# A planner for attention beside a long convolution counts TensorE's instructions in groups of 256 and holds convolution lags and fillers back by that count

## The chip, the core and the metric

The kernel runs on one core of a Trainium2 chip. A core has five engines that run their own instruction streams and meet at semaphores: TensorE (matrix multiply, PE in the profile; its weight loads are listed apart as PEld), VectorE (DVE), ScalarE (ACT), GpSimd (POOL) and SyncE (SP, used here to start DMA transfers). The metric is device microseconds (us) of one execution, lower is better. The time before is the median of three runs.

## The reference

Two independent parts are computed and laid side by side. Part A is attention over 2048 positions with 32 heads of width 16; part B is a gated convolution, in which every one of 512 channels is convolved with its own filter of 2048 taps:

```python
def _A_ref(x, wqkv, wo):            # x 2048 x 512, H = 32, Dh = 16
    qkv = (x @ wqkv)                # split into q, k, v by head
    scores = einsum("bhqd,bhkd->bhqk", q, k) * Dh ** -0.5
    o = einsum("bhqk,bhkd->bhqd", softmax(scores), v)
    return o.reshape(B, S, D) @ wo

def _B_ref(q, k, v, shift_k, ssm_k, ssm_D):   # each 2048 x 512
    k_shift = sum over t < 4 of k delayed by t, times shift_k[:, t]
    kv = k_shift * v
    y = causal convolution of kv with ssm_k, channel by channel (by FFT)
    return q * (y + kv * ssm_D)

out = concatenate([a, b], axis=-1)            # 2048 x 1024, bf16
```

## The kernel before

**Attention.** The scores are cut into 2048 blocks of 128 keys by 512 queries of one head. A score matmul (line 676) makes one block in a PSUM bank; it uses 32 of the 128 rows of the array, so up to four of different rows run together. The planner's unit of time is a step T: the score matmuls of two or three blocks, and one ScalarE instruction (line 709) that takes the exponential of those blocks at once and writes them to the ring PT. Some of the blocks, 277 of the 2048, take another way: VectorE makes their exponentials from integer arithmetic in four instructions of 512 columns (lines 751, 758 twice, 763). The blocks of step T-2 are then multiplied with the values (line 792), up to four at a time in different columns of the array, into one PSUM bank. A group is 64 blocks; at its end VectorE transposes and divides (lines 853 to 873).

**The convolution.** A channel's filter is laid in SBUF as 128 shifted copies (ring WR, 16 slots of 512 KB, filled by SP's DMAs from a scratch in HBM). Four channels form a "quad"; 128 quads of 16 lags each are computed. One lag is four small matmuls with 128 columns (line 962), one for each channel, which run together in four column strips of the array. So a lag is eight TensorE instructions, four weight loads and four matmuls, and all lags together are 8192 matmuls.

**Other work on TensorE.** Projections of x (q units, line 395; k units, 404; v units, 427), the short convolution (416), output projection (903), transposes of the convolution's result (987), and fillers (1167), matmuls with a zero weight that add nothing and that keep TensorE busy where it would wait. A q unit makes the queries of one head group and 512 positions: two halves of two matmuls, an eviction by VectorE to the single buffer QS (line 443), and eight small DMAs from POOL's queue that spread QS into the ring QT (line 260, 16 KB each). The eviction of the next q unit waits for these eight, as it overwrites QS.

**What sets the order.** The order of every engine's instructions is fixed when the kernel is built, by a planner written in Python in the same file. Each engine is an object `Eng` with a clock `t`; `Eng.op` adds an instruction (or a run of them), moves the clock by a modelled duration, and notes when its result will be there. `dma` does so for transfers, with a rate (`DMA_KB`) and a latency (`late`). The main loop goes step by step: `emit_qk` (scores and exponential of T), `pv_step` (value products), `emit_bg` (units and convolution lags), `warm_up` (fillers). In `emit_bg` a number of lags is placed that is the least of `LAGS`, a budget `st["lags"]` that grows with planned time (`PACE`, `RATE`), and what fits before the next scores are due (`room`). In `warm_up` fillers are placed up to a modelled gap. The planner's clock before the change knows of engines, semaphores and transfers, and of nothing else.

Of the kernel before, what the change touches and what calls it, by code (L numbers as in the profile page):

```python
# [23 lines left out]
C = 512  # L24
# [9 lines left out]
CHB = 32  # L34
PVB = 6
BGB = 7
N_OPEN = 68
LAGS = 6
PACE = 1.2
KEYS0 = 256  # L40
END = 16

# [16 lines left out]
T_DVE = 6  # L61
SLOT = 16
OPEN = 80
CLOSE = 10
REST = 3
LEN = 3
WIN_D = 2
S_U = 0.5
S_FX = 0.55
S_T = 0.2  # L70
S_C = 0.3
PLAN = 705
JOIN = 0.05
JOIN2 = 0.15
MOST = 3
# [7 lines left out]
BACKLOG = 6.0  # L83
MARGIN = 0.35
SPARE = 0
DMA_KB = 396
X_KB = 200
WINDOW = 3.4
HALF = 0.25
TURN = 0.1  # L90
SOON = 0.5
NEAR = 0.2
FULL = 1.6
BUSY = 0.85
FILL_GAP = 0.2
RATE = 3.7
CAP = 14.0
WAIT = 1.5
LATE = 0.2
# [2 lines left out]
SWITCH = 0.105  # L102
LANDS = 0.115
MM = 0.216
LAG = 0.0555
FILL = 0.054


class Eng:

    def __init__(self, sem, done):
        self.sem = sem
        self.n = 0
        self.ops = []
        self.seen = {}
        self.done = done
        self.t = 0.5
        self.runs = []
        self.kind = None
# [7 lines left out]
    def op(self, fn, deps=(), inc=True, us=(0.06, 0.12), run=0.0, kind=None, lat=0.132):  # L127
        if kind is None:
            self.t = max(self.t + us[0], self.at(deps) + us[1])
        else:  # L130
            self.t = max(self.t + self.turn(kind), self.at(deps) + lat) + run
            self.kind = kind
            self.runs.append((self.t, run))
        waits = []
        for d in deps:
            if d is None:
                continue
            sm, v = d
            if self.seen.get(id(sm), 0) < v:
                self.seen[id(sm)] = v  # L140
                waits.append((sm, v))
        if inc:
            self.n += 1
        self.ops.append((waits, fn, self.sem if inc else None))
        if inc:
            self.done[(id(self.sem), self.n)] = self.t + (LANDS if kind else 0.0)
        return (self.sem, self.n)

    def run(self, e):
        for waits, fn, sm in self.ops:  # L150
            for w in waits:
                e.wait_ge(*w)
            ins = fn(e)
            if sm is not None:
                ins.then_inc(sm, 1)


class DmaSem:
# [10 lines left out]
def bass_concat_heads__mha_block__ssm_conv_h3__prompt_kernel(  # L169
# [17 lines left out]
    def enter(cm):  # L187
        ctxs.append(cm)
        return cm.__enter__()

    def sem(name):
        return enter(nc.semaphore(name))
# [50 lines left out]


    done = {}
    pe, act, dve, pool, sp = [Eng(sem(n), done) for n in ("s_pe", "s_act", "s_dve", "s_pool", "s_sp")]
    dma_t = [0.0]

    def at(*deps):
        return pe.at(deps)  # L250

    def dma(eng, dsem, outp, inp, deps=(), transpose=False, kb=512, rate=DMA_KB, late=3.6):
        h = dsem.add()
        start = max(eng.t, at(*deps))
        dma_t[0] = max(dma_t[0], start + late) + kb / rate
        done[(id(h[0]), h[1])] = dma_t[0]

        def fn(e):
            f = e.dma_start_transpose if transpose else e.dma_start
            f(outp, inp).then_inc(dsem.sem, 16)  # L260
        issue = kb / (rate if rate < DMA_KB else 155) if transpose else 0.55
        eng.op(fn, deps, inc=False, us=(issue, issue + 0.06))
        return h
# [297 lines left out]
    def take_banks(T):  # L561
# [7 lines left out]
        def comes_free(b):  # L569
            if held.get(b) == "w" and (part[0] or T <= win["stop"] and (T < win["begin"] + 2 or near(T, CLOSE))):  # L570
                return False
# [14 lines left out]
        else:  # L586
# [3 lines left out]
            banks = list(range(ends[1], 6))  # L590
        if T >= N_OPEN and near(T, OPEN) and T >= win.get("last", 0) + REST and "bank" not in win and len(banks) > 2 and late["bank"] is None and len(queue) > LAST_BLKS + 18:
            b = hold(T, banks, "w")
# [21 lines left out]
    late = {"bank": None}  # L614
# [108 lines left out]
    def dve_block(T, bl):  # L723
        if len(bl) < 3 or WIN_D and "bank" in win and (part[0] or WIN_D > 1 and near(T, CLOSE)) or T < T_DVE or len(queue) < LAST_BLKS + 3 * (TAIL_GAP - N_LAST) + 3:
            return None
# [281 lines left out]
    units = [("kv", c, i) for c in range(2) for i in range(4)] + [(x, 1, i) for i in range(4) for x in "kv"]  # L1007
    early += [(N_OPEN - 5 - 2 * (len(units) - i), u) for i, u in enumerate(units)]

    def step(n):  # L1010
        return PLAN * n // (NQB * NG)

# [6 lines left out]
    part = [None]  # L1019

    def room(T):
        lim = at(h_exp[min(T, end[0] - 1)]) - 0.47 - MARGIN
        return lim - max(pe.t, at(bank_free[BGB]))

    def next_unit(T):
        if T < N_OPEN:
            return early[0] if early and ready(early[0][1]) else None
# [8 lines left out]
    def unit_step(T):  # L1036
        if T < N_OPEN:
            stop = N_OPEN
        elif "bank" in win:
# [4 lines left out]
        while not tight:  # L1044
# [3 lines left out]
            else:  # L1048
# [3 lines left out]
                due, u = job  # L1052
            if T < N_OPEN:
                bank = PVB if u == ("v", 0, 0) else BGB
# [36 lines left out]
    def emit_bg(T):  # L1091
        st = state
        unit_step(T)
        if T == N_OPEN:
            assert not early
            st["started"], st["t"] = True, pe.t
        if T - end[0] in tail_mm:
            assert st["qd"] == C // 4 and not st["turn"], (T, st)
            for t, g in tail_mm[T - end[0]]:
                op_mm(NQB - 1, t, g, g + 1, tail_bank(t))  # L1100
            return
        if st["qd"] == C // 4 and not st["turn"]:
            if T < end[0] + min(tail_mm) and h_wop[0] is not None:
                bank_free[BGB] = pe.op(keep_busy, [bank_free[BGB], h_wop[0]], run=MM, kind="F")
            return
        if st["turn"] and st["qd"] == C // 4:
            if T < end[0] + min(tail_mm) - 1 and at(h_ybw[0]) > pe.t - 0.2:
                return
            conv_turn(C // 32 - 1, BGB)
            st["turn"] = False  # L1110
            return
        if not st["started"]:
            return
        left_us = max(1.14 * (PLAN - END - T), 1.0)
        st["lags"] = min(st["lags"] + min(PACE * st["left"] / left_us, RATE) * (pe.t - st["t"]), CAP)
        st["t"] = pe.t
        left = min(LAGS, int(st["lags"]), int((room(T) - pe.turn("C") - SWITCH) / LAG))
        while left > 0 and st["qd"] < wr_next[0] and kv_n[st["qd"] // 32] == 4 and at(h_wr[st["qd"]]) + WAIT <= pe.t:
            if st["turn"] and st["qd"] % 4 == 3 and st["lag"] + left >= NB:
                left = NB - 1 - st["lag"]  # L1120
                if left <= 0:
                    break
            n0 = st["lag"]
            if n0 == 0 and st["qd"] % 4 == 0 and at(bank_free[BGB]) > pe.t - 0.2:
                break
            n1 = min(n0 + left, NB)
            left -= n1 - n0
            st["lags"] -= n1 - n0
            st["left"] -= n1 - n0
            conv_lags(st["qd"], n0, n1)  # L1130
            st["lag"] = n1 % NB
            if n1 == NB:
                st["qd"] += 1
                if st["qd"] % 4 == 0:
                    st["turn"] = st["turn"] or st["qd"] % 8 == 0
                    break
# [13 lines left out]
    def warm_up(T):  # L1150
        if T < 1 or T > end[0]:
            return
        while True:
            gap = at(h_exp[T - 1]) + 0.14 - pe.t - FILL_GAP
            lately = sum(r for t, r in pe.runs[-40:] if t > pe.t - WINDOW)
            place = filler_place(pe.t + gap)
            if place is None:
                return
            bank, s, rows, c0, most, first = place
            if first:  # L1160
                gap -= max(at(bank_free[bank]) + 0.24 - pe.t, 0.0)
            k = min(int((gap - pe.turn("C")) / FILL), int((BUSY * WINDOW - lately) / FILL) + 1, most)
            if k < 1 or lately > BUSY * WINDOW:
                return
            rhs = bass.AP(tensor=IDN.tensor if hasattr(IDN, "tensor") else IDN, offset=IDN[0:1, 0:1].offset,
                          ap=[IDN[:, :].ap[0], [0, k], [1, 128]])
            pe.op(lambda e, s=s, k=k, rhs=rhs, bank=bank, rows=rows, c0=c0, first=first: e.matmul(  # L1167
                PS[32 * s:32 * s + rows, bank, c0:c0 + 128 * k], lhsT=ZW[:, 0:rows], rhs=rhs, start=first, stop=first,
                tile_position=(0, 32 * s)),
                [h_zw, h_idn, bank_free[bank] if first else None], run=FILL * k, kind="C")  # L1170

# [16 lines left out]
    T = 0  # L1188
# [19 lines left out]
    for t in range(4):  # L1208
        h = op_mm(qb, t, 3, 4, tail_bank(t))
# [55 lines left out]
```

## Time and profile before

| | |
|---|---|
| median of three runs | 836.09 us (832.76 to 840.45) |
| the profiled execution | 834.01 us, its span 832.3 us |
| TensorE matmuls, busy | 773.8 us, 13668 instructions |
| TensorE weight loads | 13668 instructions |
| VectorE, busy | 794.8 us, 1360 instructions |
| ScalarE, busy | 808.2 us, 730 instructions |
| GpSimd, busy | 78.5 us |
| instructions in all | 30664 |
| DMA | 291.41 MB, 350 GB/s over the span |

The span runs from the first to the last instruction of the program; the time of the execution holds a little more. In the profile a row of a group gives the line, engine, operation and tiles, the number of instructions, then busy time and mean duration, then the idle time of the engine just before them and what ended it. "issue" means that the engine waited for nothing that the profile shows. In the chain of waits, each piece has its start, its length and what ran.

### The profile page before, as it was taken

The numbers are of one execution on the slowest core, as the hardware profiler recorded it, in microseconds if no ns is written. First come the engines' busy times: TensorE is split into PE (matmuls) and PEld (weight loads), VectorE is DVE, ScalarE is ACT, GpSimd is POOL, SyncE is SP. The second block draws the span as 40 slices with busy tenths as digits, with TensorE's granted clock in tenths as the row PEclk, the third lists the DMA queues.
The fourth block names the chain that finished last, engine by engine and source line by source line (L and its number), as shares of the span: only waits on it lengthen the run. The fifth ranks groups of instructions, "written<-read, shape, count | busy, mean of one in ns | idle before, by whom it ended". The sixth has DMA issues, their size and how long they took to land.

```text
span 832.3 us, 30664 instructions
## 1 busy us (share of the span) xinstructions
PE 773.8 (93%) x13668; PEld 327.7 (39%) x13668; DVE 794.8 (95%) x1360; ACT 808.2 (97%) x730; POOL 78.5 (9%) x155
## 2 busy tenths in 40 slices
PE   8899999999989899999989989989999999999997
PEld 3343344444433344444443334343443333433332
DVE  4999999999999899999989989999999999999995
ACT  6999999999999999999989989999999999999997
POOL 3300320010101001000120100101002011000000
PEclk9999999999999999999999999999999999999999
DMA  9996399999999999999999999899999999999911
GB/s 240 250 309 252 110 375 408 407 393 408 394 407 408 395 400 378 407 404 375 395 372 383 355 327 353 328 377 408 394 408 383 410 390 328 388 406 358 408 57 55
DMA packets 109235, 291.41 MB, mean 350 GB/s; under 512 B 37680, under 2 KB 41648, under 8 KB 108720
## 3 DMA queue, kind: packets, MB, share of 16 engines
q1 hardware_dynamic: 102256, 280.80, 90.1%
q0 software_dynamic: 5648, 8.27, 3.2%
q8 instruction: 108, 1.77, 0.9%
q10 hardware_dynamic: 1200, 0.39, 0.2%
q14 instruction: 23, 0.19, 0.1%
HBM read 276.83 MB, written 6.42 MB: 340 GB/s over the span
## 4 chain that ended last, share of the span: by engine, by line
ACT 69%; PE 15%; DVE 11%; issue 3%; DMA 2%; POOL 0%; DVEq 0%
ACT PT L709 69%; PE PS L676 5%; DVE EH L758 4%; PE PS L962 3%; PE PS L792 3%; DVE FX L751 3%; DVE PTD L763 2%; PE PS L1167 1%; DMA QT<-QS 1%; DMA QN<-in_B_k_dram 1%; DMA xT<-in_A_x_dram 1%; PE PS L427 0%; DVE DT L853 0%; POOL QT L260 0%; PE PS L395 0%
## 5 line engine op out<-in xcount | busy, mean ns | idle before, releaser
L709 ACT ACTIVATE PT<-PS 128x1024 bf16<-128x1024 f32 (+2 forms) x725 | 805.2, 1349 | 12.9 <-PE PS L676 12.4
L676 PE MATMUL PS<-QT,KTo 32*128 32x512 bf16 x2048 | 289.6, 386 | 29.3 <-ACT PT L709 5.6
L962 PE MATMUL PS<-WR,KV 128*15 128x128 bf16 (+15 forms) x8192 | 213.0, 220 | 10.8 <-issue 10.7
L792 PE MATMUL PS<-PT,VA 128*32 128x512 bf16 x1771 | 197.6, 391 | 7.6 <-DVE DT L853 5.4
L751 DVE TENSOR_SCALAR FX<-PS 128x512 f32<-128x512 f32 x277 | 189.1, 689 | 8.6 <-PE PS L676 8.0
L763 DVE SCALAR_TENSOR_TENSOR PTD<-EH,FX 128x512 uint16<-128x512 f32 x277 | 187.5, 685 | 0.1
L758 DVE SCALAR_TENSOR_TENSOR EH<-EH 128x512 f32<-128x512 f32 x277 | 186.4, 686 | 0.0
L758 DVE SCALAR_TENSOR_TENSOR EH<-FX 128x512 f32<-128x512 uint16 x277 | 186.3, 689 | 0.0
L962 PEld LDWEIGHTS PS<-WR,KV 128*15 128x15 bf16 (+15 forms) x8192 | 143.4, 88 | 86.6 <-issue 56.0
L676 PEld LDWEIGHTS PS<-QT,KTo 32*128 32x128 bf16 x2048 | 73.4, 91 | 220.5 <-ACT PT L709 158.2
L1167 PE MATMUL PS<-IDN,ZW 128*32 128x512 bf16 (+4 forms) x517 | 134.5, 328 | 0.3 <-DVE DT L853 0.2
L260 POOL DMA_DIRECT2D QT<-QS x120 | 59.7, 505 | 489.7 <-DVE QS L443 151.6
L792 PEld LDWEIGHTS PS<-PT,VA 128*32 128x32 bf16 x1771 | 46.9, 93 | 112.7 <-issue 95.2
L792 PE MATMUL PS<-PTD,VA 128*32 128x512 bf16 x277 | 81.3, 383 | 0.3 <-DVE PTD L763 0.3
L1167 PEld LDWEIGHTS PS<-IDN,ZW 128*32 128x32 bf16 (+1 forms) x517 | 43.3, 96 | 26.2 <-issue 11.1
L853 DVE STREAM_TRANSPOSE DT<-PS 128x512 f32<-128x512 f32 x32 | 22.9, 717 | 9.1 <-PE PS L792 9.0
L976 DVE CAST YB<-PS 128x512 bf16<-128x512 f32 x32 | 22.1, 689 | 2.3 <-PE PS L1167 1.8
L792 PEld LDWEIGHTS PS<-PTD,VA 128*32 128x32 bf16 x277 | 20.1, 95 | 2.0 <-DVE PTD L763 0.6
L903 PE MATMUL PS<-WKV,OTN 128*128 128x512 bf16 x64 | 19.4, 385 | 0.3 <-DVE OTN L873 0.3
L404 PE MATMUL PS<-xT,WKV 128*128 128x512 bf16 (+1 forms) x64 | 18.4, 378 | 1.0 <-DVE KV L462 0.5
L427 PE MATMUL PS<-WKV,xT 128*128 128x128 bf16 x256 | 18.9, 221 | 0.3 <-DVE KTo L452 0.2
L395 PE MATMUL PS<-xT,WQ 128*128 128x512 bf16 x60 | 17.5, 384 | 0.0
(65 smaller groups left out, 214.1 us busy)
## 6 DMA issues: line engine op xcount, KB each, us to landing
WR<-kz_scratch SPq DMA_DIRECT2D x512, 512.0 KB, 9.5
kz_scratch<-WR SPq DMA_DIRECT2D x1, 2176.0 KB, 8.2
QN<-in_B_q_dram POOLq DMA_DIRECT2D x2, 1024.0 KB, 12.5
out_dram<-QN POOLq DMA_DIRECT2D x2, 1024.0 KB, 8.7
QT<-QS POOLq DMA_DIRECT2D x120, 16.0 KB, 5.1
out_dram<-OUTA POOLq DMA_DIRECT2D x12, 128.0 KB, 5.6
QN<-in_B_ssm_k_dram SPq DMA_DIRECT2D x1, 1024.0 KB, 8.3
OTN<-in_B_ssm_k_dram SPq DMA_DIRECT2D x1, 1024.0 KB, 9.1
```

Source lines behind the costliest of these rows:

```text
L260: f(outp, inp).then_inc(dsem.sem, 16)
L676: ins = e.matmul(PS[:, bank, :], lhsT=KTo[32 * s:32 * s + 32, OF[n_] % 2, kt * 128:(kt + 1) * 128], rhs=QT[32 * s:32 * s + 32, n_ // 2 % R ...
L709: h_exp[T] = act.op(lambda e: e.activation(PT[:, p0:p0 + n, :].rearrange("p b f -> p (b f)"), PS[:, banks[0]:banks[0] + n, :].rearrange("p ...
L751: h_f = urgent(lambda e: e.tensor_scalar(fx, PS[:, bank, :], FIX_ADD, FIX_HI, ALU.add, ALU.min), [h, h_last.get(i - R_FX)], slack=S_FX)
L758: st["h"] = dve.op(lambda e: e.scalar_tensor_tensor(eh, src, (P1, P2)[j], src, ALU.add, ALU.mult), [st["h"], h_last.get(i - R_EH)], us=us)
L763: lambda e: e.scalar_tensor_tensor(out16, eh, P3, fx, ALU.mult, ALU.add),
L792: ins = e.matmul(dst, lhsT=w, rhs=rhs, start=(k == 0), stop=(k == KT - 1), tile_position=(0, 32 * s))
L853: h_t = urgent(lambda e: e.transpose(out=dt, in_=PS[:, PVB, :]), [h, h_mul.get(n - 1)], slack=S_T, us=(0.63, 0.751))
L903: ins = e.matmul(PS[:, bank, :], lhsT=OTN[:, PAIRS.index((o, qb)), t * 128:(t + 1) * 128], rhs=WO[:, o, :], start=(o == 0), stop=(o == 3))
L962: ins = e.matmul(PS[32 * c:32 * c + NB - n, BGB, 128 * (kk % 4):128 * (kk % 4) + 128], lhsT=KV[:, qd, n:NB, c], rhs=WR[:, r + c, 128 * (NB ...
L976: hh = urgent(lambda e: e.tensor_copy(YB[:, half, :].rearrange("p (k i) -> p k i", k=4), src), [h, h_yb[0]], slack=S_C, us=V512)
L1167: pe.op(lambda e, s=s, k=k, rhs=rhs, bank=bank, rows=rows, c0=c0, first=first: e.matmul(PS[32 * s:32 * s + rows, bank, c0:c0 + 128 * k], l ...
```

## The change

A class `Tensor` takes the place of `Eng` for TensorE. It counts instructions ("words"), two for each matmul call of an operation, starting at 62, in groups ("blocks") of 256. When an operation ends a block, the planner takes it that the next block has been asked for at that moment and is there 6.3 us later (`FETCH`); an operation that ends a block before the last one asked for has landed is delayed in the model. `spare()` tells how many instructions are left in the block, less ten for each microsecond until the landing (`NEED`); when nothing is under way it is a very large number. `emit_bg` places no more lags than `spare() / 8`, and `warm_up` places no filler when `spare()` is below 2. What is counted is the calls of matmul and transpose; other instructions of TensorE's stream, such as those that only wait for a semaphore, are not.

Ten constants of the planner and the latency it allows a DMA are changed as well: at most 7 lags in a step where it was 6, faster budget, the convolution allowed two steps sooner and planned to end 8 steps before the plan's end where it was 16, DMA latency 4.2 us where it was 3.6, DMA rate 394 where it was 396, and small ones on when PSUM banks are lent to units.

The arithmetic is the same. In the built order of after there are again 2048 score matmuls, 277 blocks on VectorE, 8192 convolution matmuls; there are 722 exponential instructions where there were 725, and 498 fillers where there were 517.

```diff
-N_OPEN = 68
-LAGS = 6
-PACE = 1.2
+N_OPEN = 66
+LAGS = 7
+PACE = 1.4
-END = 16
+END = 8
-CLOSE = 10
-REST = 3
+CLOSE = 12
+REST = 2
-PLAN = 705
+PLAN = 710
-DMA_KB = 396
+DMA_KB = 394
-TURN = 0.1
+TURN = 0.2
-RATE = 3.7
+RATE = 4.2
+BLOCK = 256
+WORD0 = 62
+FETCH = 6.3
+NEED = 10.0
+class Calls:
+    def __init__(self):
+        self.n = 0
+    def matmul(self, *args, **kw):
+        self.n += 1
+        return self
+    transpose = matmul
+class Tensor(Eng):
...
+    def op(self, fn, deps=(), **kw):
+        count = Calls()
+        fn(count)
+        words = 2 * count.n
+        t0 = self.t
+        self.left = BLOCK - self.at_word % BLOCK
+        h = super().op(fn, deps, **kw)
+        if words >= self.left:
+            part = self.left / words
+            cross = self.t - (1.0 - part) * min(kw.get("run", 0.0), self.t - t0)
+            stall = max(self.lands - cross, 0.0)
+            if stall:
+                self.stalls.append((cross, stall))
+                self.t += stall
+                if kw.get("inc", True):
+                    self.done[(id(self.sem), self.n)] += stall
+            self.lands = cross + stall + FETCH
+        self.at_word += words
+        return h
+    def spare(self):
+        need = max(self.lands - self.t, 0.0) * NEED
+        return BLOCK - self.at_word % BLOCK - need if need else 10 ** 6
-    pe, act, dve, pool, sp = [Eng(sem(n), done) for n in ("s_pe", "s_act", "s_dve", "s_pool", "s_sp")]
+    pe = Tensor(sem("s_pe"), done)
+    act, dve, pool, sp = [Eng(sem(n), done) for n in ("s_act", "s_dve", "s_pool", "s_sp")]
-    def dma(eng, dsem, outp, inp, deps=(), transpose=False, kb=512, rate=DMA_KB, late=3.6):
+    def dma(eng, dsem, outp, inp, deps=(), transpose=False, kb=512, rate=DMA_KB, late=4.2):
-        left = min(LAGS, int(st["lags"]), int((room(T) - pe.turn("C") - SWITCH) / LAG))
+        left = min(LAGS, int(st["lags"]), int((room(T) - pe.turn("C") - SWITCH) / LAG), int(pe.spare() / 8))
-            if k < 1 or lately > BUSY * WINDOW:
+            if k < 1 or lately > BUSY * WINDOW or pe.spare() < 2:
```

More of the change, by code (lines that the diff above doesn't have):

```diff
@@ L155, in run, with __init__ @@
                 ins.then_inc(sm, 1)
+class Calls:
[6 more added lines that the diff above has]
+class Tensor(Eng):
+    def __init__(self, sem, done):
+        super().__init__(sem, done)
+        self.at_word = WORD0
+        self.lands = 0.0
+        self.mean = 0.0
+    def op(self, fn, deps=(), **kw):
[17 more added lines that the diff above has]
+        return h
+    stalls = []
+    def spare(self):
+        need = max(self.lands - self.t, 0.0) * NEED
+        return BLOCK - self.at_word % BLOCK - need if need else 10 ** 6
 class DmaSem:
```

## The prediction

> **What bounds the kernel now.** I read the page's busy times and its chain of waits first, then who waited for whom, then the chain inside single stretches.
>
> ```profile
> span 832.3 us, 30664 instructions
> ...
> PE 773.8 (93%) x13668; PEld 327.7 (39%) x13668; DVE 794.8 (95%) x1360; ACT 808.2 (97%) x730; POOL 78.5 (9%) x155
> ...
> q1 hardware_dynamic: 102256, 280.80, 90.1%
> ...
> q8 instruction: 108, 1.77, 0.9%
> ...
> ACT 69%; PE 15%; DVE 11%; issue 3%; DMA 2%; POOL 0%; DVEq 0%
> ...
> L709 ACT ACTIVATE PT<-PS 128x1024 bf16<-128x1024 f32 (+2 forms) x725 | 805.2, 1349 | 12.9 <-PE PS L676 12.4
> L676 PE MATMUL PS<-QT,KTo 32*128 32x512 bf16 x2048 | 289.6, 386 | 29.3 <-ACT PT L709 5.6
> L962 PE MATMUL PS<-WR,KV 128*15 128x128 bf16 (+15 forms) x8192 | 213.0, 220 | 10.8 <-issue 10.7
> ```
>
> ScalarE is busy for 97% of the span, and 805.2 us of that are the exponentials. The change gives it the same blocks, so only its waits can go: 12.4 us in all, every one for score matmuls. What made those late is told by TensorE's own waits:
>
> ```profile
> PEld PS L676 <- ACT PT L709: 158.2, 441, 1.0
> ...
> PE PS L962 <- issue: 10.7, 11, 2.0
> ...
> PE PS L676 <- DVE QS L443: 2.4, 1, 2.4
> ...
> PE PS L792 <- issue: 1.6, 1, 1.6
> ```
>
> Ordinarily TensorE waits for ScalarE (158.2 us in 441 waits, 0.36 us each): that is its slack. Against it stand twelve long stalls that nothing in the profile releases, 10.7 + 1.6 = 12.3 us, about 1.03 us each, and one of 2.4 us for the eviction of a q unit. These thirteen, 14.7 us, are what ScalarE waits for; its rows show 12.4 because its instructions overlap:
>
> ```profile
> 624.29 191.71 ACT PT L709 x174
> ```
>
> This long undisturbed piece of the chain gives 191.71 / 174 = 1.10 us from one exponential to the next, while the mean instruction lasts 1.349 us; up to 0.25 us of a delay therefore doesn't show as idle.
>
> **Are the twelve stalls instruction fetches?** Two of them follow each other, and so I counted TensorE's instructions between them.
>
> ```profile
> 270.07 0.90 issue
> 270.97 0.22 PE PS L962
> ...
> 276.34 1.55 issue
> 277.89 0.22 PE PS L962 x2
> ```
>
> ```profile
> L962 PEld LDWEIGHTS PS<-WR,KV 128*8 128x8 bf16 (+15 forms) x95 | 1.6, 86 | 2.1 <-issue 1.8
> L676 PEld LDWEIGHTS PS<-QT,KTo 32*128 32x128 bf16 x15 | 0.5, 91 | 1.1 <-ACT PT L709 0.4 <-issue 0.4
> L1167 PEld LDWEIGHTS PS<-IDN,ZW 128*32 128x32 bf16 x5 | 0.4, 96 | 0.1
> L792 PEld LDWEIGHTS PS<-PT,VA 128*32 128x32 bf16 x11 | 0.2, 94 | 0.5 <-issue 0.5
> L792 PEld LDWEIGHTS PS<-PTD,VA 128*32 128x32 bf16 x1 | 0.1, 96 | 0.0
> ```
>
> ```profile
> L152 PEldq EVENT_SEMAPHORE  x2: 51/51/51, 271.0 to 275.0; - x2
> ```
>
> 95 + 15 + 5 + 11 + 1 = 127 weight loads, as many matmuls, and 2 instructions that only wait for a semaphore: 256. The instruction queue says the same: 1.77 MB in 108 packets is 16.4 KB each, and 2 x 13668 instructions and a few hundred waits are 108 times 256. The block from 270.97 took 6.9 us to be followed by the next, which is how long a fetch lasted there. A block that holds 15 score matmuls could be through sooner: 1.10 us for an exponential and 2048 / 725 = 2.82 score matmuls in each make 0.39 us a score matmul, so 15 are 5.9 us. The number of score matmuls in a block is thus its time at ScalarE's pace, and the many-lag blocks, with few, are those that end too soon.
>
> [...]
>
> **The change, part by part. First the count.** It counts two words for every matmul, and leaves out the waits:
>
> ```profile
> L152 PEldq EVENT_SEMAPHORE  x342: 51/51/51, 3.5 to 818.9; - x171
> ```
>
> 342 of them stand in the trace of before; the built order of after has 333 beside 27,284 counted words. So the planner's block edges agree with the true ones at the start, are half a block off in the middle of the run, a whole block off at about three quarters of it (where they agree again), and drift on. I counted score matmuls in each block of both built orders, from the eighth block to the 104th (97 blocks, the convolution's part). Blocks with at most 15: before 28; after, by the planner's own count, 9; after, by the true count, 21. With 13 or fewer: 4, 1 and 6. So the planner evens out blocks that are largely not those that are fetched. In before, 8 of the 28 blocks with at most 15 ended in one of the twelve stalls (0.29 each), and 4 of the other 69 (0.06 each; fetches that were late). By these rates after has 21 x 0.29 + 76 x 0.06 = 10.7 stalls, which at 1.03 us are 11.0 us in place of 12.3: -1.3 us. If the planner's count were the true one, it would be 9 x 0.29 + 88 x 0.06 = 7.9 stalls, 8.1 us, -4.2. I take -1.5 (the drift is small in two stretches); bounds are -12.3, if every stall goes, and the price of rival D above nothing.
>
> **The q units.** The eviction into QS waits for the DMAs of the unit before.
>
> ```profile
> 411.44 3.33 POOL QT L260 x7
> 414.77 6.72 DMA QT<-QS
> ...
> 421.62 0.70 DVE QS L443
> ...
> 422.45 0.39 PE PS L676 x3
> ```
>
> ```profile
> 420.00:432.00 12.00, 9.58 (x214) 4.69 (x212) 10.15 (x18) 9.46 (x9) 3.81 (x8) 0.86 0.99 365
> ```
>
> Eight DMAs were issued from 411.44, the last landed at 421.5, and VectorE, whose queue is in order, held the eviction that the next scores needed. ScalarE ran 9.46 of the 12 us from 420 to 432 (fourth pair), so 2.5 us were lost, the low clock of that stretch (0.86) included. In the built order of before, the two units end 22 score matmuls apart (8.6 us at 0.39), in after 76 apart (30 us), against about 10 us for the DMAs. The other close pair of the early part, 19 apart, is as close in after (21) and caused no wait in before. So this stall goes: -2.5 us; bounds 0 (another pair gets a slow landing) and -3.
>
> **The exponentials.** 722 in place of 725 for the same 1771 blocks:
>
> ```profile
> L709 ACT ACTIVATE PT<-PS 128x1536 bf16<-128x1536 f32 x316 | 482.0, 1579 | 8.7 <-PE PS L676 8.6
> L709 ACT ACTIVATE PT<-PS 128x1024 bf16<-128x1024 f32 x405 | 429.9, 1167 | 3.2 <-PE PS L676 2.7
> ```
>
> A block is 1579 - 1167 = 412 ns, the fixed part 343 ns, of which the overlap of 247 hides most: three fewer save 0.3 us.
>
> **What costs nothing, and its cover.** A seventh lag in a step adds four matmuls:
>
> ```profile
> 402.26 0.34 PE PS L962 x24
> ```
>
> That is 0.06 us, in front of scores that wait 0.36 us for ScalarE anyway. Lags put off are lags to be made up; the convolution ends 32 score matmuls before the last, where it was 46: 14 x 0.39 = 5.5 us later. Behind it hangs the last store of part B.
>
> ```profile
> 808.11 1.18 POOL L260 DMA_DIRECT2D out_dram<-QN  x1 [50.70 <-DVE QN L996]
> ```
>
> ```profile
> DMA to landing us min/median/max: 6.1/6.1/6.1
> ```
>
> It was there by about 815, 17 us before the end; 5.5 us of that is used. Without this cover each microsecond would count. The lower DMA rate and higher latency in the planner only shift when it lets lags begin; no convolution matmul waited long for a DMA in before (its row on the page names "issue" for 10.7 of 10.8 us), so I take 0, with 1 us either way. The bank-lending constants shift units by a step or two within the same slack: 0, with 1 us either way.
>
> **Sum.** -1.5 - 2.5 - 0.3 = -4.3 us against the profiled execution's 834.0: 829.7. That execution is 2.1 us below the median of the three runs, so I forecast 836.1 - 4.3 = 831.8 as a median.
>
> **The rivals.** B: most fetch stalls go, since even a wrong count spreads the lags. For it: 9 against 28 by the planner's count, and ends that agree in two stretches. Against: 21 by the true count. Time: -12.3 - 2.8, that is 821, or 825 with a third of the stalls left.
>
> C: the change doesn't do what it says: the stalls come from late fetches, not short blocks (4 of the 12 ended blocks of 16 or more), and stay; a q unit meets a slow landing elsewhere. Time 836, or 833 if only the q stall goes. [...]
>
> D, slower: fetches get longer. They travel on the DMA engines that the filter copies fill to 90%, and a faster lag budget packs copies and lags more tightly. Two or three bursts of seven lags fall into one true block (11 score matmuls, 4.3 us, is the least in after; 12 in before). Were fetches 0.8 us longer, blocks with 16 and 17 would join (37 in after): 37 x 0.29 + 60 x 0.06 = 14.3 stalls of 1.83 us, 26 us, 14 more than now; less 2.8 that is 847. It is slower by over 1% from a lengthening of about 0.7 us on. Against: the plan holds the DMA engines no busier over the whole, as the bytes are the same.
>
> One more price belongs to B and D. After a long gap TensorE's clock drops:
>
> ```profile
> 424.00:428.00 4.00, 4.00 (x88) 1.86 (x76) 4.00 (x7) 3.76 (x4) 2.41 (x6) 0.57 0.95 318
> 494.00:498.00 4.00, 3.43 (x57) 1.47 (x56) 2.09 (x5) 1.90 (x3) 0.00 (x0) 0.71 0.98 328
> 498.00:502.00 4.00, 3.85 (x59) 1.44 (x51) 3.05 (x7) 3.51 (x4) 0.00 (x0) 0.86 0.96 343
> ```
>
> The third number from the right is the granted clock: it fell behind the q stall and behind the longest fetch stall, and ScalarE lost another 0.5 us in 498 to 502. Fillers held back by `spare()` could open such gaps; there are 498 in after against 517, so I charge nothing, and 0.5 us for each further drop. [...]
>
> **How the numbers follow.** Forecast 0.52, B 0.20, C 0.18, D 0.10. The range takes B's upper part and C with the spread of the three runs: 823 to 840; B's lower half and D's upper part, some 0.17, stay outside. A measurement here tells 1% from no change, 827.7 and 844.5. Faster: B and the forecast's lower edge, 0.25. Slower: 0.07 of D. Within: 0.68.
>
> **What would show it.** Right: TensorE's waits on "issue" before lines of lags and value products add up to 9 to 12 us, in stalls whose blocks of 256, waits included, hold few score matmuls; no wait of TensorE for QS; ScalarE's waits at 7 to 10 us. B: issue waits under 5 us. D: over 20 us, and more low clock. I would be wrong altogether if ScalarE came to wait for VectorE's work or for the copies, of which before shows nothing.

## The result and the profile after

| | before | after |
|---|---|---|
| median, us (runs) | 832.48 (15) | 828.36 (15) |
| lowest to highest, us | 828.13 to 840.45 | 825.92 to 832.92 |
| profiled execution, us | 834.01 | 828.52 |

The ratio is 0.9941, with a 95% interval of 0.9916 to 0.9965. The ratio is estimated from all the runs and says 0.59%; the medians alone say 0.49%, 4.1 us, and the two profiled executions lie 5.5 us apart. Before was measured again with after, and its median over 15 runs lies 3.6 us below that of the three runs shown ahead of the prediction.

First the page of after: its span, the busy times, the chain of waits that ended last, the groups of exponentials, value products and lags, and the filter copies with their median time to landing.

```profile
span 826.8 us, 30549 instructions
...
PE 762.2 (92%) x13603; PEld 324.2 (39%) x13642; DVE 794.2 (96%) x1360; ACT 807.0 (98%) x727; POOL 78.7 (10%) x155
...
ACT 77%; DVE 10%; PE 9%; issue 2%; DMA 1%; SPq 0%
...
L761 ACT ACTIVATE PT<-PS 128x1024 bf16<-128x1024 f32 (+2 forms) x722 | 804.1, 1376 | 8.8 <-PE PS L728 8.3
...
L844 PE MATMUL PS<-PT,VA 128*32 128x512 bf16 x1771 | 199.7, 391 | 6.6 <-issue 3.5
L1014 PE MATMUL PS<-WR,KV 128*12 128x128 bf16 (+15 forms) x8192 | 201.6, 220 | 4.4 <-issue 4.3
...
WR<-kz_scratch SPq DMA_DIRECT2D x512, 512.0 KB, 8.4
```

The lines have moved with the new class: 709 is now 761, 676 is 728, 792 is 844, 962 is 1014. ScalarE's work is the same, and its share of the chain rose from 69% to 77%. Its waits for scores fell from 12.4 to 8.3 us. TensorE's stalls on "issue" before lags and value products, 12.3 us in twelve before, are 4.3 + 3.5 = 7.8 us, in ten:

```profile
PE PS L728 <- ACT PT L761: 14.1, 42, 0.9
PE PS L1014 <- issue: 4.3, 7, 1.2
PE PS L844 <- issue: 3.5, 3, 2.0
```

This is the view of TensorE's waits (total us, times, longest). The wait of 2.4 us for QS is gone; one of 0.3 us is left.

"issue" doesn't hold all of the fetch stalls. A wait is put down to a semaphore that came shortly before its end, and one of after, in the first row, is put down to VectorE. The other two rows, of the weight loads, show what it was: the first of three score matmuls had its weights loaded at 278.27 us, so its own waits were over, and the next instruction came only 1.57 us later, released by nothing.

```profile
PE PS L728 <- DVE PTD L815: 1.7, 1, 1.7
...
278.27 0.09 PEld L728 LDWEIGHTS PS<-QT,KTo 32*128 32x128 bf16 x1 [0.28 <-DVE FX L803]
279.93 0.09 PEld L728 LDWEIGHTS PS<-QT,KTo 32*128 32x128 bf16 x2 [1.57 <-issue]
```

This stands at a block edge, with the instructions that only wait counted (word 191 of 256, counted from the first instruction in the trace). So does a stall of before, which the rows put down to ScalarE and the chain of waits has as "484.97 0.84 issue". With these two, the fetch stalls are 13.1 us in before and 9.5 in after. A copy landed in 9.5 us (median) before, as this row of its page shows, against 8.4 above:

```profile
WR<-kz_scratch SPq DMA_DIRECT2D x512, 512.0 KB, 9.5
```

The windows show in which stretch the time was gained. A row has the stretch and its length, then the busy time and count of TensorE, its weight loads, VectorE, ScalarE and GpSimd, then clock, DMA share and GB/s. Before, then after:

```profile
100.00:405.00 305.00, 287.52 (x5727) 128.95 (x5731) 299.17 (x511) 301.82 (x276) 22.89 (x48) 1.00 1.02 396
405.00:785.00 380.00, 354.03 (x6501) 146.60 (x6493) 369.16 (x630) 371.44 (x338) 36.56 (x71) 0.99 1.00 377
```

```profile
100.00:405.00 305.00, 282.42 (x5582) 125.52 (x5589) 298.64 (x510) 300.52 (x274) 26.69 (x56) 0.99 1.02 390
405.00:785.00 380.00, 355.40 (x6634) 147.96 (x6657) 377.76 (x645) 379.88 (x344) 32.78 (x63) 1.00 1.00 382
```

From 405 to 785 us ScalarE (fourth pair) ran 379.88 us of 380 where it had run 371.44: 8.4 us more work done. From 100 to 405 it did 1.3 us less than before. The stalls agree. In the second stretch TensorE lost 9.0 us in before to the waits of the first two rows, and of such waits after has only the row below them:

```profile
PE PS L962 <- issue: 6.6, 6, 2.0
...
PE PS L676 <- DVE QS L443: 2.4, 1, 2.4
```

```profile
PE PS L1014 <- issue: 0.8, 2, 0.6
```

The fetch stalls that after still has from 100 us on lie at 106 to 405 us, one at 650 and one at 789, each at a true block edge, with the instructions that only wait for a semaphore counted (word 191 or 192 of 256, counted as above, at all nine of 0.3 us or more). That is roughly where the drift of the planner's count would put them: it is wrong by up to about half a block in the first stretch and nears a whole one, where the edges agree again, in the second. This is a tempting reading, and the second experiment takes it away.

### The profile page after: what moved, and what is told of

The parts are those of the page before. It is cut to its first block, busy times and chain, and to the rows that moved or that the text cites. A ratio compares the mean times of both kernels' runs of the same rounds, so it can differ in the third digit from the quotient of the medians.

```text
span 826.8 us, 30549 instructions
## 1 busy us (share of the span) xinstructions
PE 762.2 (92%) x13603; PEld 324.2 (39%) x13642; DVE 794.2 (96%) x1360; ACT 807.0 (98%) x727; POOL 78.7 (10%) x155
## 4 chain that ended last, share of the span: by engine, by line
ACT 77%; DVE 10%; PE 9%; issue 2%; DMA 1%; SPq 0%
ACT PT L761 77%; DVE EH L810 4%; PE PS L728 3%; DVE FX L803 2%; PE PS L1014 2%; PE PS L844 2%; DVE PTD L815 2%; PE PS L1219 1%; PE PS L468 1%; DMA xT<-in_A_x_dram 1%; DVE DT L905 0%; DVE YB L1028 0%; SPq L312 0%; DVE KV L514 0%; DVE OTN L925 0%
## 5 line engine op out<-in xcount | busy, mean ns | idle before, releaser
L844 PE MATMUL PS<-PT,VA 128*32 128x512 bf16 x1771 | 199.7, 391 | 6.6 <-issue 3.5
L1014 PE MATMUL PS<-WR,KV 128*12 128x128 bf16 (+15 forms) x8192 | 201.6, 220 | 4.4 <-issue 4.3
L1014 PEld LDWEIGHTS PS<-WR,KV 128*12 128x12 bf16 (+15 forms) x8192 | 140.6, 88 | 71.9 <-issue 42.5
L1219 PE MATMUL PS<-IDN,ZW 128*32 128x512 bf16 (+3 forms) x498 | 132.2, 334 | 0.0
L1219 PEld LDWEIGHTS PS<-IDN,ZW 128*32 128x32 bf16 x498 | 41.8, 96 | 24.1 <-issue 10.4
L955 PE MATMUL PS<-WKV,OTN 128*128 128x512 bf16 x53 | 16.9, 383 | 2.1 <-issue 1.6
L456 PE MATMUL PS<-xT,WKV 128*128 128x512 bf16 (+1 forms) x52 | 15.0, 373 | 2.9 <-issue 1.1
L447 PE MATMUL PS<-xT,WQ 128*128 128x512 bf16 x45 | 14.4, 382 | 2.4 <-issue 2.1
## 6 DMA issues: line engine op xcount, KB each, us to landing
QN<-in_B_q_dram POOLq DMA_DIRECT2D x2, 1024.0 KB, 12.4
```

The lines of the kernel that those rows point to most:

```text
L844: ins = e.matmul(dst, lhsT=w, rhs=rhs, start=(k == 0), stop=(k == KT - 1), tile_position=(0, 32 * s))
L1014: ins = e.matmul(PS[32 * c:32 * c + NB - n, BGB, 128 * (kk % 4):128 * (kk % 4) + 128], lhsT=KV[:, qd, n:NB, c], rhs=WR[:, r + c, 128 * (NB ...
```

## The experiments

Ratios are to before, measured beside each kernel on the same chip (its medians were 832.62 us beside 1 to 4, 833.22 beside 5 to 8 and 832.13 beside 9 to 12). "Short blocks" are those of 256 true instructions with at most 15 score matmuls, as in the prediction: 28 in before, 21 in after.

**1. The true count.** After, with the waits counted too:

```diff
-        words = 2 * count.n
...
         h = super().op(fn, deps, **kw)
+        words = 2 * count.n + max(len(self.ops[-1][0]) - 1, 0)
```

> After, with the instructions that only wait for a semaphore counted too (one word each), all constants as in after. Blocks of 256 with at most 15 score matmuls, true count, eighth to 104th block: 10 (after 21, before 28). My theory (the count works, and is blunted by the words it leaves out): 10 x 0.29 + 87 x 0.06 = 8.1 fetch stalls, about 8.4 us by the rates of the prediction, no wait for QS (the q units end at least 42 score matmuls apart from the fourth on): some 2.5 us below after, 6.5 below before, about 826. Rival 'the constants made the gain': same as after, 828. Rival 'spreading by a wrong count already takes all there is': same as after, 828.

826.11 us (12 runs), ratio 0.9929 (0.9903 to 0.9954), with 10 short blocks. TensorE's waits:

```profile
PE PS L728 <- ACT PT L761: 16.7, 52, 1.0
...
PE PS L1014 <- DMA WR<-kz_scratch: 1.8, 3, 0.9
...
PE PS L728 <- issue: 0.5, 1, 0.5
```

The rows of lags on "issue" are gone from among the longer waits: where the planner counts what is fetched, one wait of 0.5 us on "issue" is left among them. In their place lags wait 1.8 us for copies, which neither before nor after did. The gain over after lies within the intervals of the two, so the better diagnosis did not become a time that could be told apart.

**2. The constants without the count.** After, with all its constants and its DMA latency, but a planner that sees no fetch:

```diff
-            stall = max(self.lands - cross, 0.0)
+            stall = 0.0
...
-        need = max(self.lands - self.t, 0.0) * NEED
-        return BLOCK - self.at_word % BLOCK - need if need else 10 ** 6
+        return 10 ** 6
```

> After without the count: the constants and the DMA latency of after, but no limit on lags and fillers by words, and no fetch in the planner. Blocks with at most 15 score matmuls: 24. The q units that collided in before end 57 score matmuls apart. My theory: the q stall goes (-2.5 us), fetch stalls nearly as in before, 24 x 0.29 + 73 x 0.06 = 11.3, 11.7 us: 829 to 831, between the two kernels, above after. Rival 'the constants made the gain': as after, 828, with issue waits of TensorE as low as in after. Rival 'faster lags without the count hurt': 834 or more.

827.33 us (10 runs), ratio 0.9949 (0.9927 to 0.9971). My theory missed and the rival held: the whole gain is there without the count, and with 24 short blocks.

```profile
PE PS L843 <- issue: 3.6, 3, 2.7
...
PE PS L1013 <- issue: 2.1, 4, 0.7
...
PE PS L727 <- issue: 1.1, 2, 0.8
```

TensorE's longer waits on "issue" are 6.8 us here and 7.8 in after; with the fetch stalls that stand under other names they are 8.2 (one of 1.4 us at 415 us is put down to ScalarE) and 9.5. So the count as it was built, wrong by the waits, adds nothing that these runs can see to what the constants do. The good stretch of after is not its doing either: from 405 to 785 us ScalarE ran 377.77 us here.

**3. Two buffers for QS.** Before, in the same planned order, with the eviction of a q unit no longer waiting for the DMAs of the last one, but for those of the one before it (the small tile PAT is laid into DTN to make room):

```diff
-    QS = sb("QS", [128, QB])
+    QS = sb("QS", [128, 2, QB])
...
-            hh = urgent(lambda e: e.tensor_scalar(QS[:, :], PS[:, bank, :], QSCALE, None, ALU.mult),
+            hh = urgent(lambda e: e.tensor_scalar(QS[:, p % 2, :], PS[:, bank, :], QSCALE, None, ALU.mult),
...
+                        real=[h] + [h_q[2 * (p - 2) + i] if p > 2 else None for i in range(2)])
```

> Before with two buffers QS in turn, so that an eviction waits for the DMAs of the unit before the last; the order of every engine's instructions is that of before. My theory: the wait of TensorE for the eviction of QS (2.4 us) and the low clock behind it go, the fetch stalls stay at about 12 us: 2.5 us below before, about 830. Rival 'the q stall hides another wait that comes in its place': less than 1 us below before.

832.82 us (12 runs), ratio 0.9993 (0.9963 to 1.0024): the 830 expected was missed, and no gain shows. But the interval reaches from 3.1 us of gain to 2.0 of loss, so a gain of 2.5 us isn't excluded. The wait itself is gone. Its old place lies in the stretch from 405 to 500 us, first of before, then of this kernel:

```profile
405.00:500.00 95.00, 86.23 (x1503) 35.30 (x1495) 87.48 (x149) 89.13 (x82) 13.88 (x26) 0.96 1.00 365
```

```profile
405.00:500.00 95.00, 88.75 (x1613) 36.57 (x1614) 92.73 (x160) 93.88 (x87) 13.88 (x26) 1.00 1.01 381
```

ScalarE (fourth pair) ran 4.75 us more of it: the wait is gone, a fetch stall of 2.0 us at 494 us has become one of 0.2, and the granted clock is 1.00 in place of 0.96. Some of it came back just behind the old place, from 430 to 490 us, where this kernel has these two waits and before has neither, though it has the fetch stall of 0.84 us at 485 us that this kernel doesn't have:

```profile
PE PS L963 <- issue: 0.8, 2, 0.7
...
PE PS L963 <- DMA WR<-kz_scratch: 0.6, 1, 0.6
```

So in this one execution the wait was not handed on in full. What was gained there had been lost at the start: in the first 100 us ScalarE ran 89.96 us, where in before it ran 93.61. In its chain the first 12 projections took 2.75 us (first fence), in that of before 1.50:

```profile
6.00 2.75 PE PS L538 x12
```

```profile
5.63 1.50 PE PS L537 x12
```

What the wait is worth over many executions stays open.

**4 and 5. Small copies.** Before (4) and after (5), with all copies from the 17th quad on cut to an eighth of their columns, so that the rest of the convolution reads stale filters:

```diff
+                dst = WR[:, 4 * i + c, :]
+                if qd >= R_W:
+                    src = bass.AP(tensor=kz_ap.tensor, offset=kz_ap[4 * qd + c, 0].offset, ap=[[1, 128], [1, S // 8]])
+                    dst = WR[:, 4 * i + c, 0:S // 8]
-                h_wr[qd] = dma(sp, d_wr[i], WR[:, 4 * i + c, :], src, [h_kzw[0], dep])
+                h_wr[qd] = dma(sp, d_wr[i], dst, src, [h_kzw[0], dep])
```

> Before, with the copies of the filter from the 17th quad on cut to the first eighth of their columns: the convolution reads old columns, its result is left wrong, and the order of all instructions is that of before. The DMA engines are nearly idle in the convolution's part. My theory (the issue stalls are fetches that wait behind these copies): TensorE's issue waits of 12 us fall below 3, the q stall goes as its DMAs land sooner, 13 to 15 us below before: 817 to 820. Rival 'the stalls are of TensorE's issue itself, not of a transfer': issue waits stay at 12 us, 830 (only the q stall goes).

> After, with the copies of the filter from the 17th quad on cut to the first eighth of their columns, as was done to before in the run before this (820.7 us, no fetch stall left); the convolution's result is left wrong, the order of all instructions is that of after. Theory A (what the change gains, it gains in fetch stalls): with the fetches out of the way the two orders take the same time, 820 to 821. Theory B (it gains by a schedule that waits less elsewhere, and the fetch stalls are as costly as before): 4 us below, 816 to 817. In between, the shares are read from it.

820.73 us (4 runs), ratio 0.9863 (0.9829 to 0.9898) for 4, and 821.56 us (4 runs), 0.9870 (0.9844 to 0.9896) for 5. The order of every engine is that of before and of after; only bytes are gone, and the first 64 copies are whole. The page's chain and copies of 4, and the middle of its span:

```profile
ACT 93%; DVE 3%; DMA 2%; PE 2%; SPq 0%; issue 0%
...
WR<-kz_scratch SPq DMA_DIRECT2D x448, 64.0 KB, 2.9
```

```profile
200.00:700.00 500.00, 477.14 (x9052) 202.61 (x9044) 497.68 (x850) 499.63 (x457) 45.84 (x91) 1.00 0.27 60
```

The DMA share is 0.27, ScalarE ran 499.63 of 500 us, and no wait on "issue" is left among TensorE's longer ones. (In 5 there are two, 2.3 us, at 107 and 163 us, while whole copies still run; the stall that after has at 280 us is gone.) The blocks are as short as they were: the same 28 short blocks came with 12.3 us of stalls on "issue" beside whole copies (before, DMA share 1.01 from 200 to 700 us) and with none among the longer waits beside small ones (0.27). The copies cost before 12 us by this (832.62 less 820.73), a better order can regain no more than that of their price, and the change has regained about a third of it; with small copies the two orders can't be told apart.

**6. The edges moved.** Before, with 64 matmuls of one column more in a routine at the start, 128 words, so that every later block edge lies half a block elsewhere and the plan is otherwise the same:

```diff
-        for par in range(2):
+        for par in [0] * 64 + [0, 1]:
```

> Before, with 64 more matmuls of one column ahead of the first projection, where TensorE waits for x; everything else stands in the order of before, but the edges of the blocks of 256 fall half a block later in it. Blocks with at most 15 score matmuls: 18 (before 28). If the stalls belong to the edges: those of before at 187.8, 236.5, 271.0, 277.9, 494.6 and 554.4 us are gone, others stand at the new edges, some 18 x 0.29 + 79 x 0.06 = 10 of them, 10 us, 0 to 2 us below before: about 831. If they belong to the work at those places, they stay where they were. The wait for QS: if it is a part of this order, 2.4 us near 422 us are there again; if it was a chance of one execution, they are not.

835.16 us (12 runs), ratio 1.0029 (1.0010 to 1.0048). Two stretches of the chain:

```profile
228.92 2.14 issue
...
417.29 5.92 DMA QT<-QS
...
423.33 0.70 DVE QS L443
...
428.06 2.24 issue
430.31 0.28 PE PS L962 x8
```

All nine of its fetch stalls (at 115.6, 121.9, 128.5, 188.7, 231.1, 430.3, 551.7, 557.6 and 715.0 us) stand at new edges, 64 matmuls earlier in the order than an edge of before; none stands where before stalled. So the stalls belong to the edges, and not to the matmuls that they delay. But this kernel has only 18 short blocks, fewer than after, and by the rates of the prediction it should have gained. Fewer stalls came, but longer ones, of up to 2.24 us in the chain, the wait for QS is there again (1.3 us), and lags wait 2.2 us for copies, which they didn't in before. Why the stalls are longer here stays open.

**7 and 8. The constants in two halves.** Before, with after's DMA model alone (7: `DMA_KB` 394, latency 4.2), and before with the other nine constants alone (8). First the edit of 7, then that of 8:

```diff
-DMA_KB = 396
+DMA_KB = 394
-    def dma(eng, dsem, outp, inp, deps=(), transpose=False, kb=512, rate=DMA_KB, late=3.6):
+    def dma(eng, dsem, outp, inp, deps=(), transpose=False, kb=512, rate=DMA_KB, late=4.2):
```

```diff
-N_OPEN = 68
-LAGS = 6
-PACE = 1.2
-END = 16
-CLOSE = 10
-REST = 3
-PLAN = 705
-TURN = 0.1
-RATE = 3.7
+N_OPEN = 66
+LAGS = 7
+PACE = 1.4
+END = 8
+CLOSE = 12
+REST = 2
+PLAN = 710
+TURN = 0.2
+RATE = 4.2
```

> Before with the planner's DMA latency (4.2 us) and rate (394) of after alone. Blocks with at most 15 score matmuls: 14. If this part of the change made the gain: 14 x 0.29 + 83 x 0.06 = 9 stalls, 9.3 us in place of 12.3, and less waiting for early transfers: 3 to 4 us below before, 828 to 829. If not: 832.

> Before with the other nine constants of after (lags, pace, rate, plan, ends, bank lending), but the old DMA latency and rate and no count. Blocks with at most 15 score matmuls: 26. If the pace constants made the gain: 827 to 828, as the constants together. If the DMA latency did: 12 stalls, 12 us, as before, 831 to 832.

7: 826.24 us (6 runs), ratio 0.9921 (0.9897 to 0.9945). 8: 832.45 us (12 runs), ratio 0.9988 (0.9971 to 1.0005). Two numbers by which the planner foresees a transfer make the whole gain of the change; the rest does nothing that shows. In 7 (first fence) lags stall on fetches less and hardly wait for copies; in 8 they wait for both:

```profile
PE PS L962 <- issue: 4.0, 6, 1.2
...
PE PS L962 <- DMA WR<-kz_scratch: 1.2, 1, 1.2
```

```profile
PE PS L962 <- DMA WR<-kz_scratch: 5.1, 6, 1.7
...
PE PS L962 <- issue: 4.5, 7, 1.4
```

**9 and 10. Rate and latency apart.** Before with `DMA_KB` 394 alone (9), and before with a latency of 5.4 us alone (10). The latency of 4.2 with the old rate was not tried.

```diff
-DMA_KB = 396
+DMA_KB = 394
```

```diff
-    def dma(eng, dsem, outp, inp, deps=(), transpose=False, kb=512, rate=DMA_KB, late=3.6):
+    def dma(eng, dsem, outp, inp, deps=(), transpose=False, kb=512, rate=DMA_KB, late=5.4):
```

> Before with the planner's DMA rate 394 in place of 396, nothing else. Blocks with at most 15 score matmuls, true count: 28, as in before; but the two q units that collided in before now end 69 score matmuls apart. If short blocks decide: as before, 832 to 833. If the q stall decides: 2.5 us below, 830. If any reordering is worth as much as the changed DMA model was: 826 to 829.

> Before with the planner's DMA latency 5.4 us in place of 3.6, rate 396 kept. Blocks with at most 15 score matmuls: 19; q units 33 apart. If a later planned landing is what gains (lags wait in the plan for copies that in truth come late): 826 to 828, with no wait of TensorE for WR. If short blocks alone decide: 10 stalls, 830 to 831. If only chance of the order: anywhere from 828 to 835.

9: 831.89 us (12 runs), ratio 0.9997 (0.9977 to 1.0017). 10: 824.13 us (6 runs), ratio 0.9900 (0.9868 to 0.9931). The latency is what gains. Every edit to the planner also makes a new order, and an order can be better by chance; but 8 and 9 are new orders too, and gained nothing. With whole copies, all five kernels planned with 3.6 us (before, 3, 6, 8, 9) took 831.89 us or more, and all seven planned with 4.2 or more (after, 1, 2, 7, 10, 11, 12) 828.36 or less. TensorE's waits in 9 and in 10:

```profile
PE PS L962 <- issue: 9.3, 11, 1.9
...
PE PS L676 <- DVE QS L443: 0.2, 1, 0.2
```

```profile
PE PS L676 <- issue: 1.1, 1, 1.1
...
PE PS L962 <- issue: 0.8, 2, 0.5
```

The page of 10 has this row for the copies:

```profile
WR<-kz_scratch SPq DMA_DIRECT2D x512, 512.0 KB, 8.5
```

Ten has 19 short blocks and three longer waits on "issue", where 6 had 18 short blocks and nine. In 9 the two q units that collided are 69 score matmuls apart and wait 0.2 us, as the prediction wanted them, and nothing is gained (at most 1.9 us by the interval): a sign, in another order, that the wait for QS had little price.

**11 and 12. The true count with other constants.** Both count as in 1. Beside the count, 11 and then 12 differ from after by these lines:

```diff
-END = 8
+END = 16
-CLOSE = 12
+CLOSE = 10
-PLAN = 710
+PLAN = 715
-FETCH = 6.3
+FETCH = 6.1
```

```diff
-N_OPEN = 66
+N_OPEN = 68
-PACE = 1.4
+PACE = 1.3
-END = 8
+END = 12
-REST = 2
+REST = 3
-PLAN = 710
+PLAN = 715
-RATE = 4.2
+RATE = 3.7
-FETCH = 6.3
-NEED = 10.0
+FETCH = 6.1
+NEED = 12.0
-    def dma(eng, dsem, outp, inp, deps=(), transpose=False, kb=512, rate=DMA_KB, late=4.2):
+    def dma(eng, dsem, outp, inp, deps=(), transpose=False, kb=512, rate=DMA_KB, late=4.6):
```

> After with the true count and other constants (end 16, bank lending 10, plan 715, fetch 6.1). Blocks with at most 15 score matmuls: 9; q units 54 apart. By the count of blocks the same as the true count before it (10 blocks, 826.1): 825 to 827.

> After with the true count, DMA latency 4.6 us, and other constants (lags may start at step 68, pace 1.3, end 12, rest 3, plan 715, rate 3.7, fetch 6.1). Blocks with at most 15 score matmuls: 5, the fewest of all; two q units end 19 apart near 400 us, as close as in before. If short blocks and late copies are what is left to gain: 823 to 825, below after and below the true count alone. If the close q units cost 2.5 us: 826 to 827.

11: 824.98 us (7 runs), ratio 0.9914 (0.9879 to 0.9949), 9 short blocks. 12: 822.14 us (6 runs), ratio 0.9878 (0.9848 to 0.9909), 5 short blocks. Twelve beats both kernels: its interval ends below after's 0.9916 to 0.9965. It stands 1.4 us above kernel 4, whose copies are cut to an eighth. ScalarE's and TensorE's waits in 12:

```profile
PE PS L1014 <- issue: 2.5, 5, 0.8
...
ACT PT L761 <- PE PS L728: 3.0, 6, 1.0
```

Which part of the gain over after is the count's and which the latency's was not separated: the intervals of 10 and 12 overlap.

## Why the prediction was right in the total and wrong in a step

**The total.** A gain of 0.59% was measured where -4.3 of 836.1, 0.51%, was forecast, and no change of 1% came of it, as the likeliest case had it. B (most stalls go), C (nothing happens) and D (fetches get longer) did not occur. That the total came so close is luck: the first term of the sum priced the count, which adds nothing that shows (2), and the DMA model, put at 0, carries the gain (7). The median itself was forecast as 831.8 and came out as 828.36, since the three runs it was reckoned from lay 3.6 us above the median of all 15.

**The stalls are instruction fetches: right.** They move with the block edges (6) and vanish with the copies (4), and in the stretch that the prediction counted, from 270.97 to 277.89 us, the instruction queue moved one of its 108 packets. The 6.9 us given there for a fetch are the time from one edge to the next; when that packet was asked for is not shown. They were thirteen and not twelve: the one of 0.84 us at 485 us ended a block of 14 score matmuls. C's view that short blocks do not decide has a part of the truth, below.

**The planner's count is off by the waits: right, and its price was not the term.** Counting truly clears nearly all stalls (1). I gave the count -1.5 us; the stalls on "issue" fell by 12.3 - 7.8 = 4.5, all fetch stalls by 13.1 - 9.5 = 3.6. With after's constants and no count they come to 8.2 (2), so it is not the count that took them, and the term should have been about 0.

**The failed step** is the sentence "The lower DMA rate and higher latency in the planner only shift when it lets lags begin; no convolution matmul waited long for a DMA in before ... so I take 0, with 1 us either way." The two numbers alone give a ratio of 0.9921 (7), some 6.6 us of 833.2; a longer latency alone gives 0.9900 (10), the rate alone 0.9997 (9). I had looked for waits on copies, found none, and concluded that the date of a lag's start was free. But that date also decides when lags come in a run and when copies are let go, and the fetch stalls are there beside whole copies (13.1 us in before) and not beside small ones (4). The time goes with TensorE's waits: those on "issue" (rows with a longest of 0.4 us or more), on filter copies and on QS add up to 14.7 us in before and 14.5 in 6 (profiled at 834.0 and 834.5), to 9.6 to 11.4 in 8, 9 and 3 (830.4 to 833.2), 6.6 to 8.1 in 7, 2 and after (825.7 to 828.5), 1.9 to 2.5 in 10, 1 and 12 (822.5 to 825.4), and nothing in 4 (820.6). How the latency shortens them is seen in two signs and not settled. Blocks get more even (28 short ones become 19 in 10); and copies land sooner, 9.5 us (median) in before and 8.5 in 10, with 9.1 to 9.8 in the kernels of 831.9 us or more with whole copies, and 8.3 to 9.0 in those of 828.4 or less. Whether a queue with fewer copies in it lets the fetch through sooner is only argued from this; no run shows it by itself, and it stays open.

**The q stall: right that it goes; that 2.5 us go with it is not shown.** It comes and goes with the order (2.4 us in before, 1.3 in 6, 0.3 in after, 0.2 in 9). Without it the median was the same (3), with an interval that holds both 0 and 2.5 us, and 9 gained nothing without it. The prediction asked only how far apart the q units end, and not what would be late next.

**Short blocks as a measure: incomplete.** They are neither needed, as 4 of the 12 stalls that I had counted ended longer blocks, nor enough: 19 of them with three stalls (10), 18 with nine and a slower kernel (6), and 24 at after's time (2). The rates 0.29 and 0.06 were a fit to one kernel in which the length of the fetch was as it was. That the length is the other half is my estimate and not shown; that the change moved it through a constant is a guess from the landings above.

**The other zeros held.** Bank lending, lags in a step, the budget and the later end are together 0.9988 (8). So did the clock's: no further drops came. Behind after's longest stall, in the chain,

```profile
787.25 1.98 issue
```

the granted clock of the stretch fell as it had in before, to 0.84 (third from the right):

```profile
785.00:796.00 11.00, 8.85 (x158) 3.52 (x150) 8.03 (x14) 8.44 (x8) 0.00 (x0) 0.84 0.42 168
```

The other drop of after stands behind the fetch stall at 280 us (0.57 from 281 to 285 us); before had two as well, behind the q stall (0.57 from 424 to 428 us) and the fetch stall at 494 us (0.71 from 494 to 498). That "ScalarE's waits" would be 7 to 10 us and "issue" 9 to 12 came out as 8.3 and 7.8, or 9.5 with the stall at 280 us.

## What to carry to other kernels

When a planner fixes the order of the work, try its few numbers on transfers first and by themselves: here the DMA model, and in 10 its latency alone, did all that a new mechanism was credited with, and the edit that carries both says nothing of either. Where TensorE stops and nothing in the profile releases it, count its instructions to the next such stop, weight loads and instructions that only wait included: here 256 of them lay between two stops (270.97 and 277.89 us in before), and those were fetches. Where a row names a releaser, see whether the instruction that came late waited for one at all. And what a short stall is worth can drown in the spread of the executions even when it is taken away alone: here 12 runs could not tell 2.5 us from nothing.

## What the runs showed of the hardware

With a DMA share of 0.27 from 200 to 700 us no fetch stall was left among TensorE's longer waits (kernel 4, 820.73 us); with 1.01 in the same stretch, in before, twelve stalls on "issue" took 12.3 us of the span. The trace of after agrees with the prediction's reading that semaphore-only instructions are words of the block: with them the nine fetch stalls of 0.3 us or more lie at word 191 or 192 of 256, and without them anywhere from word 38 to word 184.

Single executions spread less without the fetch stalls: 828.13 to 840.45 us in 15 runs of before, 820.27 to 820.86 in four of kernel 4, whose order is the same. In 5 three of four lie between 821.40 and 821.62, and one at 825.56. With so few runs of 4 and 5 the cause of the spread is not shown.

The granted clock fell behind stalls of 1.98 us (0.84 over 11 us) and of 1.57 us of the weight loads (0.57 over 4 us) in after, but not behind one of 1.72 us in before, 1.91 us of the weight loads (1.00 from 554 to 558 us). So the length of a stall alone did not decide it, as the prediction's "After a long gap TensorE's clock drops" would have it. And the same 12 projections at the start took 1.50 us in one profiled execution and 2.75 in another, with a granted clock of 1.00 in the rows of both; what made that is not shown.
